# A token loop on one core: turning y on VectorE, and the float32 products of a chunk in two groups instead of four

## The chip, the cores and the metric

The program runs on one core of a Trainium2 chip. A core has TensorE (PE: matrix products, with PEld for its weight loads), VectorE (DVE), ScalarE (ACT), GpSimd (POOL) and SyncE (SP, which here only issues DMAs). Each engine works through its own instructions strictly in order and waits at an instruction until the semaphores that it needs are set. The metric is the time of one execution on the device in microseconds (us), the median of several runs.

## The reference

Three stages follow each other; x has 8 sequences of 3072 rows of 256 numbers, so 24576 tokens in all.

```
X = rfft(x over the sequence);  Y = shrink(X @ (w_r + i w_i) + b);  y = irfft(Y)      # y: 24576 x 256
h = y @ w_in                                   # 24576 x 2048
t = (h - tanh(h)) @ w_out                      # 24576 x 256
logits = t @ phi                               # 24576 x 32
d = softmax of logits over all tokens;  slot_input = d.T @ t
slot_out[e] = relu(slot_input[e] @ w1[e]) @ w2[e]      # 8 experts, 4 slots each
out = (softmax of logits over the slots) @ slot_out
```

## The kernel before, in words

**Three phases.** The spectral phase takes the first 700 us or so, the token phase then runs to about 2150 us, the expert phase is the rest. The change lies in the token phase.

**The token phase.** The 24576 tokens are taken in 48 chunks of 512. `w_out` is never applied to a single token: with g = tanh(h) the logits are sums of products of g and of y with folded weights (`wp`, `wy`), and slot_input is built from d.T @ g and d.T @ y, over all chunks, with a running maximum (`acc`, `accy`, `ssum`). For each chunk c the steps have short names in the table `PLAN` (lines 29 to 42), which sets the order of everything by hand; an entry is (name, offset of the chunk, arguments), and every engine gets its instructions in that order.

- `P` w n (`wino`, line 749): h is computed by a Winograd scheme, for each of four weight blocks w in seven products n = 1 to 7. One product is six matmuls (of split float32, `f32r`, three terms for each of two halves). Products 1, 6, 7 and 4 of a block add up one after the other in the same PSUM bank, and after each of the four ACT copies the bank to an SBUF tile `g` (line 782) before the next one may write to the bank. Product 2 has a bank of its own, 5 and 3 share a third. A bank is a tile `ph`; there are six.
- `A` (`add`, line 784): DVE adds a bank to a part of g (line 789). `G` (`gate`): ACT takes the tanh of a whole g tile of 128x1024 (line 793).
- `T` (`turn_g`, line 840): DVE transposes g in 32x32 blocks (line 846) into a tile `gt`, two instructions per g tile. `reg` (`regroup`, line 852): 16 DMAs from SP carry one half of a chunk's `gt` (h = 0 or 1) to four tiles `gq`, so that the tokens lie on the partitions.
- `L` p (`logit_mm`, line 885): plain float32 matmuls of g tiles p and p+1 with `wp` into the bank `pl` (line 892), and at p = 6 also those of y with `wy` (line 900).
- `TY` kk (`turn_y`, line 805): y is turned by PE, four 128x128 transposes (line 812) into the bank `pd` for each of two halves, and ACT copies the bank to the tile `yq` (line 813). `loadr` loads y again for this (tile `yr`).
- `sum`, `sum2`, `max`, `exp`, `turnexp`: the logits' maximum and exponentials; `comb`, `cexp`, `cend`: the softmax over the slots, stored by a DMA.
- `DY` and `D` (`dy_mm`, `dg_mm`): plain float32 matmuls of the turned exponentials `et` with `yq` (line 828) and with `gq` (line 1020). `accy` and `acc` add them up on DVE.

**What a chunk's turn of the plan contains.** The entries with offset -1 belong to the chunk before. In one turn PE has 28 products (168 matmuls), and among them four groups of plain float32 matmuls: L2 and L4; then L6 with y, and TY0; then TY1, and L0 of the next chunk; then DY and D. SP's DMAs come in this order: the load of y for the next chunk, the store of the softmax, the 16 DMAs of the second half (h = 1) of the chunk before, `loadr`, and the 16 DMAs of the first half (h = 0) of this chunk. Those write to `gq` tiles that D reads, and so wait in part for D.

Of the kernel before, what the change touches and what calls it, by code (L numbers as in the profile page):

```python
# [9 lines left out]
F32 = mybir.dt.float32  # L10
# [3 lines left out]
ALU = mybir.AluOpType  # L14
# [4 lines left out]
S, D = 3072, 256  # L19
# [7 lines left out]


PLAN = (
# [8 lines left out]
    ("reg", -1, 1), ("W", 0, 3), ("splitt", 1, 0), ("comb", -1), ("P", 0, 3, 7),  # L38
# [3 lines left out]
)  # L42
TOKENS_BESIDE = {-4: 1, -2: 1, 0: 1, 1: 2, 2: 3, 3: 4}
# [590 lines left out]
def token_phase(tc, nch, yd, wh, wl, wp, wy, ident, ew):  # L634
# [8 lines left out]
    nc = tc.nc  # L643
    with ExitStack() as ctx:
# [73 lines left out]
        gt = {}  # L718
        banks = count()

        def bank():
            k = next(banks) % (4 if ps2 is None else 6)
            return (ps if k < 4 else ps2).tile([128, 512], F32, tag=f"b{k}", name="ph")
# [71 lines left out]
        yr = {}  # L795
        yq = {}
# [23 lines left out]
        def dy_mm(c):  # L820


            beside = c < nch - 1
            o = dy[c] = lp[c + 1][:, 256:320] if beside else bank()[:, 0:64]
            y = yq.pop(c)
            for k in range(4):
                for a in (3, 2, 1, 0):
                    nc.tensor.matmul(  # L828
                        o[32 * a:32 * a + 32], ex[c][:, k, :], y[:, a, k], start=k == 0 and not beside, stop=k == 3,
                        skip_group_check=True,  # L830
                    )

        def accum_y(c):
# [3 lines left out]
            else:  # L837
                nc.vector.tensor_copy(accy, o)

        def turn_g(c, p):  # L840
            g = gs[c, p]
            if (c, p // 4) not in gt:
                gt[c, p // 4] = gtp.tile([128, 16, 8, 32], F32, tag="gt", name="gt")
            t = gt[c, p // 4]
            for u in range(2):
                nc.vector.transpose(out=t[:, :, 2 * (p % 4) + u, :], in_=g[:, u, :].rearrange("p (c i) -> p c i", i=32))  # L846

        gq = {}

        gl = {}  # L850

        def regroup(c, h):

            t = gt.pop((c, h)).rearrange("p (k q) f i -> p q k (f i)", q=4)
            if h == 0:
                gq[c] = [ew.gq_tile([128, 4, 512]) for _ in range(4)]
            for a in range(4):
                o = gq[c][a][:, :, 256 * h:256 * h + 256]
                for q in range(4):
                    nc.sync.dma_start(out=o[32 * q:32 * q + 32], in_=t[32 * a:32 * a + 32, q])  # L860

        def turn_pe(c, p, engines):

            if p // 4 not in gl:
                gl[p // 4] = gtp.tile([128, 4, 4, 256], F32, tag="gt", name="gl")
            o = gl[p // 4].rearrange("p k a (f i) -> p k f a i", i=32)
            for u in range(2):
                t = bank()
                for k in range(4):
                    k = slice(128 * k, 128 * k + 128)  # L870
                    nc.tensor.transpose(t[:, k], gs[c, p][:, u, k], ident)
                src = t.rearrange("p (k a i) -> p k a i", k=4, a=4)
                dst = o[:, :, 2 * (p % 4) + u]
                if engines[u] is nc.scalar:
                    nc.scalar.activation(dst, src, AF.Copy)
                else:
                    engines[u].tensor_copy(dst, src)
# [51 lines left out]
        ex = {}  # L929
# [34 lines left out]
        def turn_exp(c):  # L964
            e, rs, a = le[c][64:128], rss.pop(c), al.get(c)
            et = sp.tile([128, 4, 32], F32, tag="et", name="et", bufs=1)
            for r in range(2):
                nc.vector.transpose(
                    out=et[64 * r:64 * r + 64].rearrange("p k s -> p (k s)"), in_=e[:, 128 * r:128 * r + 128]
                )  # L970
            if c:
                nc.vector.scalar_tensor_tensor(
                    out=ssum[0:64], in0=ssum[0:64], scalar=a[0:64], in1=rs, op0=ALU.mult, op1=ALU.add
                )
                nc.vector.tensor_copy(a[64:128], a[0:64])
            else:
                nc.vector.tensor_copy(ssum[0:64], rs)
            ex[c] = et
# [31 lines left out]
        def dg_mm(c):  # L1010

            o = dp[c] = ps2.tile([128, 512], F32, tag="d", name="pd")
            if c < nch - 1:
                parts = [(slice(0, 512), gq.pop(c))]
            else:
                parts = [(slice(256 * h, 256 * h + 256), [gl[h][:, :, a] for a in range(4)]) for h in range(2)]
            for f, g in parts:
                for k in range(4):
                    for a in (3, 2, 1, 0):
                        nc.tensor.matmul(  # L1020
                            o[32 * a:32 * a + 32, f], ex[c][:, k, :], g[a][:, k], start=k == 0, stop=k == 3
                        )
            del ex[c]
# [14 lines left out]
        gtp = ew.gtp  # L1038
# [5 lines left out]
        def do(name, k, *args):  # L1044
            if (name, k, *args) not in done:
                done.add((name, k, *args))
                calls[name](k, *args)
# [2 lines left out]
            "P": wino, "A": add, "G": gate, "T": turn_g, "L": logit_mm, "D": dg_mm, "acc": accum, "sum": sum_l,  # L1050
            "sum2": sum_l2, "max": soft_max, "exp": soft_exp, "turnexp": turn_exp, "comb": combine,
            "cexp": combine_exp, "cend": combine_end, "loady": load_y, "rawt": raw_t, "splity": split_y,
            "lowy": low_y, "splitt": split_t, "reg": regroup, "loadr": load_raw, "TY": turn_y, "DY": dy_mm,
            "accy": accum_y,
        }

        def chunk(c):

            for name, d, *args in PLAN:
                k = c + d  # L1060
                if name == "S":

                    if c == 1:
                        split_sw(*args)
                elif name == "W":
                    if c == nch - 1:
                        weights(*args)
                elif k > 0 and k < nch or k == 0 and name not in "PAG":
                    if k < nch - 1 or name not in ("T", "reg"):
                        if c < nch - 1 or name not in ("D", "DY", "accy"):  # L1070
                            do(name, k, *args)
                    if c == 1 and (name, k, *args) == ("L", 0, 4):
                        do("L", 0, 6)

        def weights(w):

# [17 lines left out]
        c = 0  # L1094
        for s in range(8):
            p = FIRST[s]
            if s == 3:
                ew.open_mid()
            if s == 5:
                ew.open_late()  # L1100
                acc, accy, ssum = ew.acc, ew.accy, ew.ssum
# [33 lines left out]
        c = nch - 1  # L1135
# [59 lines left out]
class ExpertWeights:  # L1195
# [61 lines left out]

    def load_ct(self, c0, c1):
        n = c1 - c0
        u = self.gtp.tile([128, n, 128], F32, tag="gt", name="ect") if c0 else self.gq_tile([128, n, 128])  # L1260
        for c in range(c0, c1, 16):
            m = min(c + 16, c1)
            self.tc.nc.sync.dma_start(out=u[:, c - c0:m - c0], in_=self.ctd[:, c:m])
        for c in range(c0, c1, 8):
            self.cts[c] = u[:, c - c0:c - c0 + 8]
# [5 lines left out]
    def pieces(self, j, home):  # L1271
        def tile(pool, tag, n=1024, **kw):
            t = pool.tile([128, n], F32, tag=tag, name="ewt", **kw)
            return [t[:, 512 * i:512 * i + 512] for i in range(n // 512)]
# [9 lines left out]
        if home[0] == "s":  # L1284
            return tile(self.tyq, home, 1536)
        if home == "gt":
            r = tile(self.gtp, "gt", 4096)
            self.spare["gt"] = r[4:]
            return r[:4]
        if home == "gq":  # L1290
            t = self.gq_tile([128, 2048])
# [205 lines left out]
```

## Time and profile before

| | |
|---|---|
| median of 3 runs | 2262.81 us (2259.74 to 2264.0) |
| the profiled execution | 2261.4 us, of which the span is 2259.6 us |
| mean granted TensorE clock | 0.993 |
| PE, DVE, ACT, POOL busy | 98%, 78%, 64%, 29% of the span |
| DMA packets, share of 16 engines | 77.6% |

A share is an average over the whole span. The profile says what one execution did; busy PE counts modelled ends of pipelined matmuls, so two matmuls that follow each other at 0.12 us each show 0.28 us. What a matmul costs is therefore read from the distance of starts, or from a whole piece of the chain.

### The profile page before, as it was taken

To read this page: it belongs to the slowest core of one execution; us is meant where nothing else is said; L and a number is where in the kernel's file an instruction comes from. 1 tells how busy PE (TensorE), PEld (TensorE's weight loads), DVE (VectorE), ACT (ScalarE), POOL (GpSimd) and SP (SyncE) were. 2 spreads that over 40 slices of the span, in tenths; PEclk is the share of its full clock that TensorE was granted. 3 is DMA by queue.
4 is the path that set the end of the run, shared out by engine and by line. 5 is a ranking of instruction groups with operands and counts; after the bars stand their busy time and mean duration, and the time that the engine had idled before them with its cause. 6 is when DMAs were issued, how large, how long until landed. Compare 5 with 4: busy or idle time off the path is not lost.

```text
span 2259.6 us, 51262 instructions
## 1 busy us (share of the span) xinstructions
PE 2210.0 (98%) x19832; PEld 1819.3 (81%) x19832; DVE 1764.8 (78%) x3557; ACT 1456.5 (64%) x2395; POOL 656.5 (29%) x666
## 2 busy tenths in 40 slices
PE   6999999999999999999999999999999999999989
PEld 3678888887888888888888888888888888888747
DVE  3999988988995787787777877877778778777634
ACT  2456666666556677777766777676767676767524
POOL 1334333443443322222222222222222222222111
PEclk8999999999999999999999999999999999999999
DMA  8778899898657777777777777778777777777899
GB/s 227 233 226 264 250 267 277 245 261 269 201 186 211 179 168 178 179 181 181 184 172 176 175 178 179 178 180 189 171 177 177 175 179 177 182 186 173 243 341 366
DMA packets 404019, 471.17 MB, mean 209 GB/s; under 512 B 36160, under 2 KB 351808, under 8 KB 403392
## 3 DMA queue, kind: packets, MB, share of 16 engines
q1 hardware_dynamic: 403664, 467.85, 77.6%
q8 instruction: 157, 2.57, 0.5%
q14 instruction: 86, 0.70, 0.1%
q10 hardware_dynamic: 112, 0.04, 0.0%
HBM read 164.45 MB, written 106.17 MB: 120 GB/s over the span
## 4 chain that ended last, share of the span: by engine, by line
PE 87%; DVE 5%; DMA 4%; issue 2%; SPq 1%; ACT 0%; POOL 0%; DVEq 0%; POOLq 0%; ACTq 0%
PE ph L771 41%; PE pl L892 8%; PE pd L1020 8%; PE pmix L322 5%; PE pi L407 4%; PE pf L248 4%; PE pf L281 3%; PE p_out L1319 3%; PE pi L379 3%; PE pa L322 2%; PE pd L812 2%; DMA ewt<-in_moe_w 1%; PE pl L828 1%; DVE sw L372 1%; PE pl L900 1%
## 5 line engine op out<-in xcount | busy, mean ns | idle before, releaser
L782 ACT ACTIVATE g<-ph 128x512 f32<-128x512 f32 x752 | 448.0, 596 | 379.5 <-PE ph L771 354.5
L789 DVE TENSOR_TENSOR g<-ph,g 128x512 f32<-128x512 f32 x564 | 373.3, 676 | 157.7 <-PE ph L771 147.2
L846 DVE STREAM_TRANSPOSE gt<-g 128x512 f32<-128x512 f32 x752 | 476.2, 681 | 13.0 <-DMA gq<-gt 6.5
L771 PE MATMUL ph<-th,s 128*128 128x256 f32 x2256 | 482.0, 286 | 2.1 <-ACT g L782 2.1
L771 PEld LDWEIGHTS ph<-th,s 128*128 128x128 f32 x2256 | 377.8, 189 | 41.4 <-issue 19.4
L793 ACT ACTIVATE g<-g 128x1024 f32<-128x1024 f32 x376 | 392.2, 1053 | 1.5
L771 PE MATMUL ph<-tl,s 128*128 128x256 f32 x1128 | 318.3, 282 | 0.0
L771 PE MATMUL ph<-y,wh 128*128 128x256 f32 x1128 | 316.4, 280 | 0.0
L771 PE MATMUL ph<-yh,wl 128*128 128x256 f32 x1128 | 315.7, 280 | 0.0
L771 PE MATMUL ph<-yh,wh 128*128 128x256 f32 x1128 | 315.7, 280 | 0.0
L684 POOL TENSOR_TENSOR tl<-tr,th 128x512 fp32r<-128x512 f32 x94 | 121.8, 1297 | 383.8 <-ACT th L683 350.3
L372 POOL TENSOR_TENSOR sw<-t,c 64x256 f32<-64x256 f32 x192 | 169.5, 883 | 170.1 <-DVE c L364 131.3
L771 PEld LDWEIGHTS ph<-tl,s 128*128 128x128 f32 x1128 | 213.9, 190 | 0.0
L771 PEld LDWEIGHTS ph<-yh,wh 128*128 128x128 f32 x1128 | 212.8, 189 | 0.1
L771 PEld LDWEIGHTS ph<-yh,wl 128*128 128x128 f32 x1128 | 212.4, 188 | 0.0
L771 PEld LDWEIGHTS ph<-y,wh 128*128 128x128 f32 x1128 | 212.3, 188 | 0.1
L678 POOL TENSOR_TENSOR tr<-y 128x256 f32<-128x256 f32 x92 | 67.8, 737 | 470.3 <-DMA y<-yd 470.3
L892 PE MATMUL pl<-g,wp 128*32 128x256 f32 x3072 | 195.4, 383 | 0.0
L1020 PE MATMUL pd<-gq,et 128*32 128x512 f32 x1504 | 183.8, 598 | 2.1 <-DMA gq<-gt 2.1
L669 POOL TENSOR_TENSOR y<-y,yh 128x1024 fp32r<-128x1024 f32 x46 | 110.6, 2403 | 182.9 <-issue 182.8
L407 PEld LDWEIGHTS pi<-i,v 96*128 96x128 f32 x1024 | 127.5, 191 | 26.0 <-issue 20.8
L281 PEld LDWEIGHTS pf<-f,a 128*128 128x128 f32 x768 | 102.5, 195 | 54.3 <-issue 40.9
(225 smaller groups left out, 4586.0 us busy)
## 6 DMA issues: line engine op xcount, KB each, us to landing
gq<-gt SPq DMA_DIRECT2D x1504, 128.0 KB, 2.5
xt<-in_x SPq DMA_DIRECT2D x64, 384.0 KB, 5.4
vd<-vs SPq DMA_DIRECT2D x96, 256.0 KB, 3.3
v<-vd SPq DMA_DIRECT2D x64, 384.0 KB, 5.4
yd<-yt SPq DMA_DIRECT2D x48, 512.0 KB, 5.6
y<-yd SPq DMA_DIRECT2D x48, 512.0 KB, 4.9
yr<-yd SPq DMA_DIRECT2D x48, 512.0 KB, 3.7
a<-ad SPq DMA_DIRECT2D x47, 512.0 KB, 6.0
```

The costliest lines, as they stand in the source:

```text
L281: nc.tensor.matmul(p[:, :, h, gg, :], t[:, gg, 128 * h:128 * h + 128], f2[:, 128 * g:128 * g + 128], start=True, stop=True,)
L322: nc.tensor.matmul(o, st[u], w[m], start=first and k == 0, stop=last and k == 2)
L372: eng.tensor_tensor(out=v[64 * ri:64 * ri + 64, gg], in0=t[q, e], in1=c[q, e], op=ALU.subtract)
L407: nc.tensor.matmul(p[:, a, :], t[:, 4 * u + a, :], i2[:, 96 * n2:96 * n2 + 128], start=True, stop=True)
L684: nc.gpsimd.tensor_tensor(out=lo, in0=t, in1=hi.bitcast(F32), op=ALU.subtract)
L771: nc.tensor.matmul(o[:, 256 * j:256 * j + 256], a[u][:, 128 * j:128 * j + 128], y[v], start=new and j == 0 and k == 0, stop=n in (2, 3, 4) ...
L782: nc.scalar.activation(e[n], o.rearrange("p (j n) -> p j n", j=2), AF.Copy)
L789: nc.vector.tensor_tensor(out=h, in0=o, in1=h, op=ALU.add)
L793: nc.scalar.activation(g, g, AF.Tanh)
L846: nc.vector.transpose(out=t[:, :, 2 * (p % 4) + u, :], in_=g[:, u, :].rearrange("p (c i) -> p c i", i=32))
L892: nc.tensor.matmul(lp[c][q:q + 32, 0:256], wp[:, 2 * p + f, :], half_of(gs[c, p + f // 2][:, f % 2], h), start=p == 0 and f < 2, stop=Fals ...
L1020: nc.tensor.matmul(o[32 * a:32 * a + 32, f], ex[c][:, k, :], g[a][:, k], start=k == 0, stop=k == 3)
```

## The change

`turn_y` is no longer called in the loop (it stays for the last chunk). A new step `TD` (`turn_yr`) transposes y on DVE in 32x32 blocks into two more places of the tile `gt` of the second half, which grows from 8 to 10 places; the second half's 16 DMAs carry 320 instead of 256 numbers a row, and `DY` reads its y from the tail of the `gq` tiles. The two `gt` tiles get names and one buffer each, where they took turns in two buffers. In the plan L2, L4 and L6 now stand together behind product (1, 2), and L0 stands directly ahead of DY and D. One `scalar_tensor_tensor` on a 64x1 operand becomes a `tensor_scalar`. The SBUF space that is put aside for dynamic DMAs is set to 1024.

```diff
 PLAN = (
-    ("P", 0, 0, 6), ("cend", -2), ("L", -1, 2), ("T", -1, 4), ("T", -1, 7), ("G", -1, 6), ("loady", 1), ("W", 0, 0), ("L", -1, 4),
+    ("P", 0, 0, 6), ("cend", -2), ("T", -1, 4), ("T", -1, 7), ("TD", -1), ("G", -1, 6), ("loady", 1), ("W", 0, 0),
...
-            y = yq.pop(c)
+            if beside:
+                y = [g[:, :, 512:576] for g in gq[c]]
+            else:
+                y = [yq[c][:, a] for a in range(4)]
...
+        def gt_tile(c, h):
+            if (c, h) not in gt:
+                gt[c, h] = gtp.tile([128, 16, 8 + 2 * h, 32], F32, tag=f"gt{h}", name="gt", bufs=1)
+            return gt[c, h]
+
+        def turn_yr(c):
+
+            t = gt_tile(c, 1)
+            for kk in range(2):
+                nc.vector.transpose(out=t[:, :, 8 + kk, :], in_=yr[c][:, kk].rearrange("p (c i) -> p c i", i=32))
...
             if h == 0:
-                gq[c] = [ew.gq_tile([128, 4, 512]) for _ in range(4)]
+                gq[c] = [ew.gq_tile([128, 4, 576]) for _ in range(4)]
             for a in range(4):
-                o = gq[c][a][:, :, 256 * h:256 * h + 256]
+                o = gq[c][a][:, :, 256 * h:256 * h + 256 + 64 * h]
...
             if c:
-                nc.vector.scalar_tensor_tensor(
-                    out=ssum[0:64], in0=ssum[0:64], scalar=a[0:64], in1=rs, op0=ALU.mult, op1=ALU.add
+                nc.vector.tensor_scalar(
+                    out=ssum[0:64], in0=ssum[0:64], scalar1=a[0:64], scalar2=rs, op0=ALU.mult, op1=ALU.add
                 )
...
-                    if c == 1 and (name, k, *args) == ("L", 0, 4):
-                        do("L", 0, 6)
...
-    nc = bacc.Bacc("TRN2", target_bir_lowering=False, num_devices=1)
+    nc = bacc.Bacc("TRN2", target_bir_lowering=False, num_devices=1, dynamic_dma_scratch_size=1024)
```

**PE at the head of a turn.** Names with numbers are tiles; `ph_16653` is the bank of products 1, 6, 7 and 4 of block 0. Before, product 6, then L2 and L4 (`pl`), then the start of product 7:

```order
L771 MATMUL ph_16653<-th_16577,s_7815 128x256 [waits Activation_49]
L771 MATMUL ph_16653<-tl_16578,s_7815 128x256
L771 MATMUL ph_16653<-th_16577,s_7815 128x256 x2
L771 MATMUL ph_16653<-tl_16578,s_7815 128x256
L771 MATMUL ph_16653<-th_16577,s_7815 128x256
L892 MATMUL pl_16514<-g_16339,wp_77 32x256 [waits DVE_49]
L892 MATMUL pl_16514<-g_16339,wp_77 32x256 x3
L892 MATMUL pl_16514<-g_16383,wp_77 32x256 x4
L892 MATMUL pl_16514<-g_16394,wp_77 32x256 x4
L892 MATMUL pl_16514<-g_16482,wp_77 32x256 x4
L771 MATMUL ph_16653<-th_16649,s_7815 128x256 [waits Activation_49]
L771 MATMUL ph_16653<-tl_16650,s_7815 128x256 [waits Pool_49]
```

In the changed kernel the same place, with `ph_15610` for that bank:

```order
L771 MATMUL ph_15610<-th_15525,s_7815 128x256 [waits Activation_49]
L771 MATMUL ph_15610<-tl_15526,s_7815 128x256
L771 MATMUL ph_15610<-th_15525,s_7815 128x256 x2
L771 MATMUL ph_15610<-tl_15526,s_7815 128x256
L771 MATMUL ph_15610<-th_15525,s_7815 128x256
L771 MATMUL ph_15610<-th_15606,s_7815 128x256 [waits Activation_49]
L771 MATMUL ph_15610<-tl_15607,s_7815 128x256 [waits Pool_49]
L771 MATMUL ph_15610<-th_15606,s_7815 128x256 x2
L771 MATMUL ph_15610<-tl_15607,s_7815 128x256
L771 MATMUL ph_15610<-th_15606,s_7815 128x256
```

The 32 logit matmuls that stood between products 6 and 7 are gone from there; product 7 writes to the bank behind product 6 directly.

**PE at blocks 1 and 2.** Before, the end of product 1 of block 2 (`ph_16804`), then L6 with y and the four transposes of TY0, then product 4 of block 1, whose bank `ph_16749` product 7 of block 1 had filled ahead of these rows:

```order
L771 MATMUL ph_16804<-yh_16502,wh_85 128x256
L771 MATMUL ph_16804<-y_16311,wh_85 128x256
L771 MATMUL ph_16804<-yh_16502,wl_93 128x256
L892 MATMUL pl_16514<-g_16492,wp_77 32x256 x4
L892 MATMUL pl_16514<-g_16593,wp_77 32x256 x4
L900 MATMUL pl_16514<-yr_16662,wy_78 32x256 [waits DMAHW6_49]
L900 MATMUL pl_16514<-yr_16662,wy_78 32x256 x3
L812 MATMUL pd_16826<-ident_72,yr_16662 128x128 [waits DVE_49]
L812 MATMUL pd_16826<-ident_72,yr_16662 128x128 x3
L771 MATMUL ph_16749<-th_16649,wh_88 128x256 [waits Activation_49]
L771 MATMUL ph_16749<-tl_16650,wh_88 128x256
```

In the changed kernel the last matmul of that product 7 (`ph_15692`), product 1 of block 2 (`ph_15775`) and the start of product 4:

```order
L771 MATMUL ph_15692<-th_15606,s_7867 128x256
L771 MATMUL ph_15775<-yh_15465,wh_85 128x256 [waits DVE_49]
L771 MATMUL ph_15775<-y_15273,wh_85 128x256
L771 MATMUL ph_15775<-yh_15465,wl_93 128x256
L771 MATMUL ph_15775<-yh_15465,wh_85 128x256
L771 MATMUL ph_15775<-y_15273,wh_85 128x256
L771 MATMUL ph_15775<-yh_15465,wl_93 128x256
L771 MATMUL ph_15692<-th_15606,wh_88 128x256 [waits Activation_49]
L771 MATMUL ph_15692<-tl_15607,wh_88 128x256
```

One product of six matmuls now stands between products 7 and 4 of block 1. In the same way products 1 and 6 of block 3, which had product 5, TY1 and L0 between them, now have product 5 alone.

**DVE at the end of a turn.** Before: `accy`, the first transposes into the second half's `gt`, the last two adds of block 3, and the first row of `cend`:

```order
L836 SCALAR_TENSOR_TENSOR accy_7776<-accy_7776,al_17722,pl_17765 128x64 [waits PE_49]
L846 STREAM_TRANSPOSE gt_17897<-g_17733 128x16x32 [waits DMAHW4_49,DMAHW3_49,DMAHW5_49,DMAHW2_49,DMAHW6_49,DMAHW1_49,DMAHW7_49,DMAHW0_49,Activation_49]
L846 STREAM_TRANSPOSE gt_17897<-g_17733 128x16x32
L789 TENSOR_TENSOR g_17743<-ph_17805,g_17743 128x2x256
L789 TENSOR_TENSOR g_17743<-ph_17746,g_17743 128x2x256 [waits PE_49]
L1000 TENSOR_REDUCE cz_17959<-lt_17832 128x4 [waits Activation_49]
```

In the changed kernel, with `yr_16025` for y:

```order
L839 SCALAR_TENSOR_TENSOR accy_7776<-accy_7776,al_15840,pl_15957 128x64 [waits PE_49]
L858 STREAM_TRANSPOSE gt_16009<-g_15851 128x16x32 [waits DMAHW4_49,DMAHW3_49,DMAHW5_49,DMAHW2_49,DMAHW6_49,DMAHW1_49,DMAHW7_49,DMAHW0_49,Activation_49]
L858 STREAM_TRANSPOSE gt_16009<-g_15851 128x16x32
L789 TENSOR_TENSOR g_15861<-ph_15908,g_15861 128x2x256
L852 STREAM_TRANSPOSE gt_16009<-yr_16025 128x16x32 [waits DMAHW3_49]
L852 STREAM_TRANSPOSE gt_16009<-yr_16025 128x16x32
L789 TENSOR_TENSOR g_15861<-ph_15864,g_15861 128x2x256 [waits PE_49]
L1012 TENSOR_REDUCE cz_16073<-lt_15935 128x4 [waits Activation_49]
```

The two transposes of y stand between the two adds of block 3, and the first of them waits for the load of y.

## Rows read from the trace of the kernel before

**Rows 1.** Token phase: length, busy PE, PEld, DVE, ACT, POOL, clock, DMA share, GB/s.

```profile
740.00:2120.00 1380.00, 1380.00 (x14316) 1159.14 (x14314) 1088.94 (x2244) 975.23 (x1561) 356.54 (x317) 1.00 0.75 178
```

**Rows 2.** The chain, one turn of the plan: start us, us, what.

```profile
1498.03 3.75 PE ph L771 x30
1501.78 1.86 PE pl L892 x32
1503.64 6.58 PE ph L771 x54
1510.22 1.00 PE pl L892 x16
1511.22 0.43 PE pl L900 x8
1511.65 0.59 PE pd L812 x4
1512.24 5.68 PE ph L771 x48
1517.93 0.44 PE pd L812 x4
1518.36 1.00 PE pl L892 x16
1519.36 4.46 PE ph L771 x36
1523.83 0.58 PE pl L828 x32
1524.41 3.69 PE pd L1020 x32
```

**Rows 3.** Groups of PE by line: busy us, mean ns, idle before: TY.

```profile
L812 PE MATMUL pd<-ident,yr 128*128 128x128 f32 x376 | 58.9, 279 | 0.0
```

**Rows 4.** Timeline, PE and ACT: the end of product 6 and its copy.

```profile
1501.50 0.28 PE L771 MATMUL ph<-th,s 128*128 128x256 f32 x1
1501.81 0.60 ACT L782 ACTIVATE g<-ph 128x512 f32<-128x512 f32 x1
```

**Rows 5.** Timeline, PE and ACT: a place in the second turn where PE waited.

```profile
731.87 0.28 PE L771 MATMUL ph<-yh,wl 128*128 128x256 f32 x1
732.80 0.59 ACT L782 ACTIVATE g<-ph 128x512 f32<-128x512 f32 x1
733.44 0.38 PE L771 MATMUL ph<-th,s 128*128 128x256 f32 x1 [1.29 <-ACT g L782]
733.66 0.28 PE L771 MATMUL ph<-tl,s 128*128 128x256 f32 x1
```

**Rows 6.** Timeline, ACT in blocks 1 and 2: tanh, copies, the logits' copy.

```profile
1510.05 1.05 ACT L793 ACTIVATE g<-g 128x1024 f32<-128x1024 f32 x1
1511.00 0.59 ACT L782 ACTIVATE g<-ph 128x512 f32<-128x512 f32 x1
...
1512.77 0.37 ACT L920 ACTIVATE le<-pl 64x256 f32<-64x256 f32 x1
1513.03 0.59 ACT L782 ACTIVATE g<-ph 128x512 f32<-128x512 f32 x1
```

**Rows 7.** The page: DVE's transposes, all turns.

```profile
L846 DVE STREAM_TRANSPOSE gt<-g 128x512 f32<-128x512 f32 x752 | 476.2, 681 | 13.0 <-DMA gq<-gt 6.5
```

**Rows 8.** Timeline, DVE: the changed small operation, and the second add of block 3.

```profile
1520.35 0.99 DVE L972 SCALAR_TENSOR_TENSOR ssum<-ssum,al,rs 64x1 f32<-64x1 f32 x1
...
1530.45 0.69 DVE L789 TENSOR_TENSOR g<-ph,g 128x512 f32<-128x512 f32 x1 [2.12 <-PE ph L771]
```

**Rows 9.** Timeline, SP: the second half's 16 DMAs.

```profile
1507.31 11.22 SPq L860 DMA_DIRECT2D gq<-gt  x16
```

**Rows 10.** The page: DMA issues, last the us from issue to landing.

```profile
gq<-gt SPq DMA_DIRECT2D x1504, 128.0 KB, 2.5
```

**Rows 11.** The same view, 1.5 us with only regrouping DMAs.

```profile
1501.00:1502.50 1.50, 1.50 (x23) 1.11 (x25) 0.72 (x5) 1.40 (x4) 0.46 (x1) 1.00 0.88 208
```

More of the change, by code (lines that the diff above doesn't have):

```diff
@@ L828, in dy_mm @@
                     nc.tensor.matmul(
-                        o[32 * a:32 * a + 32], ex[c][:, k, :], y[:, a, k], start=k == 0 and not beside, stop=k == 3,
+                        o[32 * a:32 * a + 32], ex[c][:, k, :], y[a][:, k], start=k == 0 and not beside, stop=k == 3,
                         skip_group_check=True,
@@ L838, in accum_y @@
                 nc.vector.tensor_copy(accy, o)
+        def gt_tile(c, h):
[6 more added lines that the diff above has]
+                nc.vector.transpose(out=t[:, :, 8 + kk, :], in_=yr[c][:, kk].rearrange("p (c i) -> p c i", i=32))
         def turn_g(c, p):
             g = gs[c, p]
-            if (c, p // 4) not in gt:
-                gt[c, p // 4] = gtp.tile([128, 16, 8, 32], F32, tag="gt", name="gt")
-            t = gt[c, p // 4]
+            t = gt_tile(c, p // 4)
             for u in range(2):
@@ L864, in turn_pe @@
             if p // 4 not in gl:
-                gl[p // 4] = gtp.tile([128, 4, 4, 256], F32, tag="gt", name="gl")
+                gl[p // 4] = gtp.tile([128, 4, 4, 256], F32, tag=f"gt{p // 4}", name="gl", bufs=1)
             o = gl[p // 4].rearrange("p k a (f i) -> p k f a i", i=32)
@@ L1013, in dg_mm @@
             if c < nch - 1:
-                parts = [(slice(0, 512), gq.pop(c))]
+                parts = [(slice(0, 512), [g[:, :, 0:512] for g in gq.pop(c)])]
             else:
@@ L1052, in token_phase @@
             "cexp": combine_exp, "cend": combine_end, "loady": load_y, "rawt": raw_t, "splity": split_y,
-            "lowy": low_y, "splitt": split_t, "reg": regroup, "loadr": load_raw, "TY": turn_y, "DY": dy_mm,
+            "lowy": low_y, "splitt": split_t, "reg": regroup, "loadr": load_raw, "TY": turn_y, "TD": turn_yr, "DY": dy_mm,
             "accy": accum_y,
@@ L1068, in chunk @@
                 elif k > 0 and k < nch or k == 0 and name not in "PAG":
-                    if k < nch - 1 or name not in ("T", "reg"):
+                    if k < nch - 1 or name not in ("T", "TD", "reg"):
                         if c < nch - 1 or name not in ("D", "DY", "accy"):
                             do(name, k, *args)
-                    if c == 1 and (name, k, *args) == ("L", 0, 4):
-                        do("L", 0, 6)
         def weights(w):
@@ L1259, in load_ct @@
         n = c1 - c0
-        u = self.gtp.tile([128, n, 128], F32, tag="gt", name="ect") if c0 else self.gq_tile([128, n, 128])
+        u = self.gtp.tile([128, n, 128], F32, tag="gt1", name="ect", bufs=1) if c0 else self.gq_tile([128, n, 128])
         for c in range(c0, c1, 16):
@@ L1286, in pieces @@
         if home == "gt":
-            r = tile(self.gtp, "gt", 4096)
+            r = tile(self.gtp, "gt0", 4096, bufs=1)
             self.spare["gt"] = r[4:]
```

10 rows, old and new, of the table PLAN are left out of this document.

## The prediction, made before the changed kernel was run

> **What bounds the kernel now.** I read the busy time by stage first. In 1380 us of the token phase PE is busy for 1380, DVE for 1089, ACT for 975 [rows 1], so PE is the bound there and has no gap that another engine could fill or open. Next the chain: over one turn of the plan, from 1498.03 to 1524.41 + 3.69 = 1528.10, it is PE alone, 30.07 us [rows 2]. The reader should see four stretches of products ("ph") and between them the four groups of plain float32 matmuls. The stretch of 48 matmuls takes 5.68 us, 0.118 each, so a product of six takes 0.71; the stretches that follow a group end up longer: 3.75 for 30 is 0.20 over 30 x 0.118, and 6.58 for 54 is 0.19 over [rows 2]. That 0.19 is what PE pays to come back from a group. Whatever shortens PE's work shortens a turn, as long as PE still finds nothing to wait for; there are 376 / 8 = 47 turns with a TY [rows 3].
>
> **What the change takes from PE.** The two groups of four transposes cost 0.59 and 0.44, together 1.03 us a turn [rows 2]. With them goes one return of 0.19 (of the four, the stretch behind TY0, 5.68, shows none of its own). L2, L4 and L6 in one group may run at the 1.86 / 32 = 0.058 each of the first group where the lone groups of 16 show 1.00 [rows 2], 0.07 less for each of L6 and L0. So a turn loses between 1.03 + 0.19 = 1.22 and 1.22 + 0.14 = 1.36 us; I take 1.30. Over 47 turns that alone is 61 us.
>
> The Trainium skill, page "TensorE: Matmul & The Clock Gate", section "Part 4: PE-mode transpose", gives about 275 ns for a 128x128 transpose inside a kernel. The rows here show 279 ns for one as a duration, but four within 0.44 to 0.59 us, since they overlap [rows 2, 3]; the piece of the chain is what a turn gets back.
>
> **What the change makes PE wait for.** The groups did a second job: they stood between products that write to one bank. Product 6's result must be copied by ACT before product 7 writes to the same bank. Before, L2 and L4 (1.86 us) cover that copy; in the new order product 7 of block 0 follows product 6 directly. Its price comes from two places. The last matmul of product 6 starts at 1501.50, its copy at 1501.81 and takes 0.60 [rows 4]: the copy ends 0.91 after that start, and ACT does the same work ahead of it as before. Where PE did wait for a copy, the copy ended at 732.80 + 0.59 = 733.39, PE began at 733.44, 0.05 later, and its next matmul came at 733.66, 0.22 behind instead of 0.12 [rows 5]: 0.10 more. So product 7 in effect starts 0.91 + 0.05 + 0.10 = 1.06 after the last start, where 0.12 would do: 0.94 us lost.
>
> The same rule holds at two more places. Between products 7 and 4 of block 1 stood product 1 of block 2 and the group L6, y and TY0; now only that product, 0.71. Between products 1 and 6 of block 3 stood product 5 and the group TY1, L0; now only product 5. Each loses 0.94 - 0.71 = 0.23, if ACT is free when the bank is ready. Product 4 of block 0 still has two products and the new group behind product 7, and every other pair has two products or more, 1.42, which covers the 0.94. Sum: 0.94 + 0.23 + 0.23 = 1.40 us a turn.
>
> ACT is in order too, and the pauses of the second and third group are gone from the long stretch of 20 products. The tightest place is product 7 of block 2, which waits for product 6's copy. From the end of product 7 of block 1 to there, ACT has four copies of 0.59, two tanh of 0.95 (1510.05 to 1511.00) and the logits' copy of 0.26 (1512.77 to 1513.03) [rows 6], 4.52 us, less where neighbours overlap. With 0.31 ahead and 0.15 behind that is 4.98; PE takes 0.12 + 6 x 0.71 + 0.23 = 4.61. ACT is late by 0.37 at most, and by nothing if the copies overlap by 0.1 each as rows 6 show for the tanh (1.05 long, followed after 0.95). I take 0.10. The stretch loses no further tanh, and ACT loses two copies of y.
>
> **What DVE and the DMAs take on.** Two transposes of 0.68, 1.36 us a turn [rows 7], stand between the last two adds of block 3. The second of these waited 2.12 us for PE [rows 8], and the new work fits into that wait. They need the new load of y, which goes out right behind the second half's DMAs, at 1518.5 or so [rows 9], while they come after DY and D, towards 1528 [rows 2]. The small operation of 0.99 [rows 8] becomes cheaper by something between nothing and nearly all of it; it lies in the stretch where DVE is busiest, so it only pays for part of the transposes. Without the cover DVE would be late by up to 1.36 at the end of a turn, on the add that product 2 of block 1 waits for; four products lie in between.
>
> The second half's 16 DMAs take 11.22 us of issue from 1507.31 [rows 9], so the last goes out at 1518.53 and lands 2.5 later [rows 10], at 1521.0; DY starts at 1523.83 [rows 2]. That is 2.8 us of slack. DY came 25.8 us behind the last D; in the new order it is 19.9 of products, 0.4 of returns, 3.3 of the first group, 0.9 of L0 and 1.5 of waits, 26.0, so the slack stays (without the waits it would be 1.3 to 1.5). With 320 instead of 256 numbers a row the DMAs may cost nothing more, if issue sets their pace, or a quarter more engine time: the engines are busy for 0.88 of the issue time [rows 11], 0.88 x 1.25 = 1.10, so up to 0.10 x 11.22 = 1.1 us later. Both are inside the slack; cost nothing, with 0 to 0.3 if the landing also slows.
>
> On this the Trainium skill speaks against the change: "DMA: Bandwidth & Descriptors", section "How a descriptor splits into AXI transactions", says that an aligned descriptor becomes one transaction for each 256 B, so 1280 B would be five where 1024 B are four. By that rule the upper end of the last paragraph would hold, and the sum would still be the same; no row here shows a 1280 B row.
>
> The buffers with names of their own change nothing: each half used every second buffer before. The space for dynamic DMAs shows in no row of an engine; cost nothing.
>
> **The sum.** A turn: -1.30 + 1.40 + 0.10 = +0.20 us. Over 47 turns +9.4 us. On the profiled execution's 2261.4 us that is 2270.8, and the median of the runs lies 1.4 above that execution: 2272. The likeliest case has its own bounds: -1.36 + 1.40 = +0.04 a turn, 2 us, to -1.22 + 1.40 + 0.37 = +0.55, 26 us: 2265 to 2289.
>
> **The rivals.**
> Faster: the waits don't come, because the copy of product 6 is not waited for at the start of product 7, or ACT starts it before the product's last matmul. Then a turn keeps its 1.30, 61 us, and the time is 2202. For it: the chain shows PE without a single wait at these places [rows 2]. Against it: product 7 adds to what product 6 left in the bank while the copy needs the sum without it, and rows 5 show PE standing for 1.29 us in just such a case. It decides at the head of the turn: a wait below 0.8 there brings the sum below zero. A weaker form, half of the waits, gives -0.6 a turn, 2235.
> Faster by another price: were a transpose worth the 279 ns of its row [rows 3], eight would give back 2.23 instead of 1.03, and a turn would change by -1.00, 47 us: 2216. The page on TensorE named above, with its 275 ns, would lead there. Against it stand the pieces of 0.59 and 0.44.
> No change: the lower bound of the sum, +0.04 a turn, or up to +0.1: 2263 to 2267. ACT's overlaps then hide the place in block 2, and the groups lose their extra 0.14.
> Much slower: ACT becomes the bound in the long stretch. If a tanh comes in front of a copy at one of the two places where one product is left, 0.95 is added there, 45 us: 2317. For it: ACT's 4.5 us of work against PE's 4.6. Against it: the tanh ahead of product 7's copy in block 1 follows product 6's copy at once and has two products' time, 1.42, for its 0.95; and ahead of the other place ACT has only the short exponentials and one copy. Late DMAs at DY would be a second way, some 0.3 a turn.
>
> **How the numbers follow.** The waits with the sum of +0.1 a turn or more: 0.58. No change: 0.25. Faster, all forms: 0.12. Much slower: 0.05. No change means within 0.2%, 4.5 us, about what a measurement of this kernel can tell. Faster by over 0.2% takes the 0.12 and a little of the no-change case, 0.13; within 0.2%: 0.27; slower: 0.60. The range goes from 2257, so that it holds the no-change case and the weakest gains, to 2289, the upper bound of the likeliest case.
>
> **What would show it.** In the changed profile PE should have, in every turn, a wait on ACT's copy (line 782) of about 0.8 us in front of product 7 of block 0, and two of about 0.1 to 0.2 in blocks 1 to 3; the group of L2, L4 and L6 about 2.8 us long, with y 0.43; no "pd" with ident before the last chunk; turns of about 30.3 us; PE busy below its 1380 of 1380. DVE should show the two transposes of y with no wait for `yr` and no wait of PE on DVE; DY no wait on a DMA. The forecast is wrong if turns come out at 29 us (no waits), or if PE waits for DVE or for `gq`.

## The result, and the profile after

The changed kernel took 2286.41 us (median of 4 runs, 2280.33 to 2290.77) against 2263.4 us before (2259.74 to 2266.32): a ratio of 1.0106 with a 95% interval of 1.0090 to 1.0123, so slower by 1.1%. The forecast was 2272 us, in a range of 2257 to 2289. The direction and the range held, but the time was not spent where the forecast put it. The profiled execution took 2280.3 us (span 2278.6), the fastest of the four, 19 us more than the one before; what follows accounts for that one. All times here are medians of executions at a granted clock of 0.99; one of e8_no_copy_waits at 0.75 (2633.47 us) is left out of its figure.

The token phase by stage, as in [rows 1]; PE is now busy for 1332 of 1380 us, with DVE as busy as before:

```profile
740.00:2120.00 1380.00, 1332.31 (x13752) 1091.99 (x13744) 1094.37 (x2307) 907.16 (x1441) 354.57 (x315) 1.00 0.82 192
```

What PE waited for in that stretch (engine, line <- who: us in total, times, longest); before the list was empty:

```profile
PE ph L771 <- ACT g L782: 30.9, 45, 0.7
PE pl L831 <- DMA gq<-gt: 10.5, 10, 3.0
PE pl L831 <- DVE lt L998: 2.2, 2, 1.1
PE pl L831 <- DVE g L789: 2.1, 3, 0.8
PE pl L831 <- DVE cm L1002: 1.4, 1, 1.4
```

The first row is the forecast wait on product 6's copy, 0.69 in each of 45 turns. The others, with one of 0.4 that is not shown, are waits in front of DY, 16.6 us together. A wait for several semaphores is put down to the one that came last; the three DVE rows name transposes, a maximum and an add that DY does not read. The landings in the trace show that they are waits for `gq` too: behind 15 of the 17 waits DY starts 0.09 to 0.25 us after the last wide DMA has landed.

The chain of one quiet turn, answering to [rows 2] (start, us, what):

```profile
1503.07 3.75 PE ph L771 x30
1506.82 0.02 issue
1506.85 0.60 ACT g L782
1507.45 0.04 issue
1507.50 2.40 PE ph L771 x18
1509.89 2.73 PE pl L904 x48
1512.62 0.43 PE pl L912 x8
1513.05 15.09 PE ph L771 x120
1528.14 1.00 PE pl L904 x16
1529.14 0.49 PE pl L831 x29
1529.63 3.43 PE pd L1032 x32
```

It ends at 1533.06: 29.99 us, against 30.07 before. The four groups took 9.59 us, the two take 8.08; the stretches of products took 20.47 and take, with the wait, 21.9. So the saved work and the waits on copies cancel, 0.1 us a turn in the change's favour. But only some turns are like this. The distance from one D to the next was 29.97 to 30.21 before, in all turns but the last; now it goes from 29.95 to 33.31, and the sum over 46 turns is 22 us longer. A slow turn of the same execution shows why (SP's issues, then the chain):

```profile
1601.57 1.42 SPq L658 DMA_DIRECT2D y<-yd  x1
1603.08 12.05 SPq L872 DMA_DIRECT2D gq<-gt  x16
```

```profile
1614.36 7.65 DMA gq<-gt
1622.02 0.09 issue
1622.11 0.82 PE pl L831 x29
```

The last wide DMA goes out at 1614.36 and lands 7.65 us later, and DY starts then. The page's DMA rows, answering to [rows 10] (which has both halves in one), show the median landing of the wide DMAs and of the first half's narrow ones; a landing is counted from the start of the DMA's issue:

```profile
gq<-gt SPq DMA_DIRECT2D x752, 160.0 KB, 4.6
gq<-gt SPq DMA_DIRECT2D x752, 128.0 KB, 2.4
```

DY needs the last of the 16, and there the two kernels part. Below are the second half's first two DMAs and its last three in the turn of [rows 9], before (last number: us to landing); then the same in the slow turn above:

```profile
gq<-gt SPq DMA_DIRECT2D x2, 128.0 KB, 3.5
gq<-gt SPq DMA_DIRECT2D x3, 128.0 KB, 2.4
```

```profile
gq<-gt SPq DMA_DIRECT2D x2, 160.0 KB, 6.0
gq<-gt SPq DMA_DIRECT2D x3, 160.0 KB, 6.2
```

Over all turns of each trace, the median landing falls from 4.7 us at the first of the 16 to 2.5 at the last before, and only from 4.8 to 4.1 in the changed kernel. Both series start with a lag, right behind the load of y (0.5 MB); the narrow one works it off and the wide one does not. The issue of all 16 takes 12.63 us in the median turn and took 11.37. In the packet records of this trace's token phase (740 to 2120 us) a row of 1280 B took 94 ns (median of 92160) and one of 1024 B 71 (92672); in the kernel before the second half's rows of 1024 B took 73.

On DVE all went as hoped, answering to [rows 8]: the transposes of y fill the wait of the second add, and the small operation takes 0.27 for 0.99.

```profile
1496.15 0.27 DVE L984 TENSOR_SCALAR ssum<-ssum,al,rs 64x1 f32<-64x1 f32 x1
...
1503.34 1.28 DVE L852 STREAM_TRANSPOSE gt<-yr 128x512 f32<-128x512 f32 x2
1505.42 0.69 DVE L789 TENSOR_TENSOR g<-ph,g 128x512 f32<-128x512 f32 x1 [0.80 <-PE ph L771]
```

### The profile page after: what moved, and what is told of

Read it like the earlier page. It is cut to its first block, busy times and chain, and to the rows that moved or that the text cites. A ratio compares the mean times of both kernels' runs of the same rounds, so it can differ in the third digit from the quotient of the medians.

```text
span 2278.6 us, 50416 instructions
## 1 busy us (share of the span) xinstructions
PE 2181.9 (96%) x19456; PEld 1770.3 (78%) x19456; DVE 1786.2 (78%) x3651; ACT 1403.9 (62%) x2301; POOL 657.0 (29%) x666
## 4 chain that ended last, share of the span: by engine, by line
PE 46%; SPq 9%; DMA 6%; DVE 5%; ACT 2%; issue 1%; DVEq 0%; ACTq 0%
PE ph L771 29%; SPq L872 8%; PE pd L1032 7%; PE pl L904 5%; DMA gq<-gt 3%; PE p_out L1329 3%; DVE gt L858 2%; DMA ewt<-in_moe_w 2%; PE pl L831 1%; DVE g L789 1%; ACT g L782 1%; PE pl L912 1%; DMA gq<-wo 0%; SPq L1018 0%; ACT g L793 0%
## 5 line engine op out<-in xcount | busy, mean ns | idle before, releaser
L904 PE MATMUL pl<-g,wp 128*32 128x256 f32 x3072 | 185.9, 382 | 0.0
L1032 PE MATMUL pd<-gq,et 128*32 128x512 f32 x1504 | 173.2, 595 | 0.0
```

The lines of the kernel that those rows point to most:

```text
L904: nc.tensor.matmul(lp[c][q:q + 32, 0:256], wp[:, 2 * p + f, :], half_of(gs[c, p + f // 2][:, f % 2], h), start=p == 0 and f < 2, stop=Fals ...
L1032: nc.tensor.matmul(o[32 * a:32 * a + 32, f], ex[c][:, k, :], g[a][:, k], start=k == 0, stop=k == 3)
```

## The experiments

Two theories stood against each other. The DMA theory: the wide DMAs land late, and DY waits for them. The rival: VectorE (or ScalarE) is late in the new order, or the waits on copies are the price.

**e1_narrow: the wide DMAs taken away.** From the changed kernel:

```diff
-gq[c] = [ew.gq_tile([128, 4, 576]) for _ in range(4)]
+gq[c] = [ew.gq_tile([128, 4, 512]) for _ in range(4)]
-o = gq[c][a][:, :, 256 * h:256 * h + 256 + 64 * h]
+o = gq[c][a][:, :, 256 * h:256 * h + 256]        # and the source cut to 0:256
-y = [g[:, :, 512:576] for g in gq[c]]
+y = [g[:, :, 0:64] for g in gq[c]]
```

Expected: 

> The changed kernel with the second half's DMAs back at 256 numbers a row and gq tiles of 512; DY reads 64 columns of g in place of y, so that y's share of slot_input is left out. VectorE still turns y, the plan is untouched. DMA theory (the wide DMAs land late and DY waits for them in some turns; the waits on product copies and the saved work on TensorE cancel to -0.1 us a turn): no wait in front of DY, turns of 29.97 us throughout, 2263 - 5 - 2 = 2256 us (2250 to 2262). Rival (VectorE with 1.36 us more a turn is late at the end of a turn, TensorE waits for it): the DMAs' width changes nothing, 2280 to 2287 us.

Measured: 2271.01 us, 1.0045 of before (1.0030 to 1.0061). No wait in front of DY is left, nor in front of D, which is the one that needs the second half's DMAs here, as DY reads columns of the first half. All turns but the last are 30.19 to 30.30 us long. What PE still waits for is product 6's copy, 30.9 us in 45 waits up to 2100 us, as in the changed kernel.

The rival falls: VectorE does the same work and nobody waits for it. But the time is 15 us above what the DMA theory gave, 11 of them because a turn is 30.21 and not 29.97. The chain shows the piece that differs, D, 3.67 where the changed kernel has 3.43:

```profile
1527.76 1.00 PE pl L904 x16
1528.76 0.45 PE pl L831 x32
1529.21 3.67 PE pd L1032 x32
```

**e2_before_wide: the wide DMAs alone, in the kernel before.** Its plan and TensorE's turning of y stay; `TD` and the 320 numbers are added, with the changed kernel's `gt` tiles and space for dynamic DMAs, which e1 has too:

```diff
-("A", 0, 3, 2), ("P", 0, 3, 3)
+("A", 0, 3, 2), ("TD", 0), ("P", 0, 3, 3)
-o = gq[c][a][:, :, 256 * h:256 * h + 256]
+o = gq[c][a][:, :, 256 * h:256 * h + 256 + 64 * h]
```

Expected: 

> The kernel before, its plan and TensorE's turning of y kept, and added to it VectorE's two transposes of y at the end of a turn and the second half's DMAs with 320 numbers a row (what they carry of y is not read). TensorE's work and order are those of before. DMA theory: the last wide DMA lands about 4 us later than the narrow one did, against 2.8 us of slack at DY and 3.3 at D, so D waits for gq in a good part of the turns: 2268 to 2295 us. Rival (VectorE late, only in the new order): the transposes fit into the 2.1 us wait, 2262 to 2266 us, no wait at D.

Measured: 2288.99 us, 1.0123 (1.0102 to 1.0144). Quiet turns stay at 30.07, others reach 32.64, and PE waits at D (up to 2100 us):

```profile
PE pd L1029 <- DMA gq<-gt: 16.4, 15, 2.4
```

The wide DMAs alone cost as much as the whole change. VectorE's transposes are in this kernel too, but e1 has them without the DMAs and without a wait.

**e3_moved: the wait on product 6's copy taken away.** From the changed kernel:

```diff
-("G", -1, 6), ("loady", 1), ("W", 0, 0),
+("G", -1, 6), ("loady", 1), ("W", 0, 0), ("L", -1, 2), ("L", -1, 4), ("L", -1, 6),
-("P", 0, 1, 2), ("L", -1, 2), ("L", -1, 4), ("L", -1, 6), ("P", 0, 0, 4)
+("P", 0, 1, 2), ("P", 0, 0, 4)
```

Expected: 

> The changed kernel with L2, L4 and L6 moved from behind product (1, 2) to between products (0, 6) and (0, 7); all else the same. The wait of 0.69 us (0.94 with the return) on product 6's copy must go. DMA theory: TensorE comes to DY about 0.9 us earlier in every turn and waits there for the wide DMAs instead, so at most a third of 43 us is gained: 2270 to 2286 us, waits in front of DY of 25 to 60 us in sum. Rival (the copy wait is the price): all of it is gained, 2286 - 43 = 2243 us (2236 to 2252).

Measured: 2291.43 us, 1.0127 (1.0098 to 1.0156): nothing gained. The copy wait is gone; the waits in front of DY grew from 15.6 to 45 us (both up to 2100 us), of which these are the largest:

```profile
PE pl L831 <- DMA gq<-gt: 21.2, 20, 2.9
PE pl L831 <- DVE lt L998: 8.5, 8, 1.2
PE pl L831 <- DVE cm L1002: 7.1, 5, 1.6
```

Not all of this is TensorE coming earlier. With the group ahead of product 7, the add that waits for product 7's copy comes later on VectorE, and so do the transposes behind it that the wide DMAs carry: the first wide DMA goes out 11.0 us after D's end instead of 10.3 (medians over the turns), 0.03 us behind the end of a transpose. So the edit also delayed the DMAs by some 0.7 us a turn, and how much of the 0.94 it would gain without that was not tried.

**e4_narrow_moved: both edits together.**

Expected: 

> Both edits together: DMAs of 256 numbers (DY reads 64 columns of g, y's share of slot_input is left out) and L2, L4, L6 between products (0, 6) and (0, 7). DMA theory: with the DMAs out of the way TensorE's side shows in full: turns of 29.97 - 0.94 = 29.03 us, 2256 - 43 = 2213 us (2206 to 2224). Rival (VectorE late): no better than 2240 us.

Measured: 2226.12 us, 0.9844 (0.9826 to 0.9862). Turns are 29.25, 0.96 below e1's. So the copy wait is worth 0.96 a turn, as forecast (0.94), once the DMAs are out of the way, and nothing in e3, where they are in it. Of the 13 us above the expected 2213, 11 are again D's 3.67. What is left in the long stretch of products:

```profile
1515.90 17.22 PE ph L771 x138
1533.12 1.00 PE pl L904 x16
1534.12 0.45 PE pl L831 x32
1534.57 3.67 PE pd L1032 x32
```

138 x 0.118 and the return of 0.19 make 16.5; 0.70 are short waits. The starts of the matmuls show where. In the changed kernel's quiet turn product 4 of block 1 loses 0.26 us, product 6 of block 3 0.24 and product 7 of block 2 0.18, each behind a copy by ACT: 0.68 for the prediction's 0.23, 0.23 and 0.10.

**e8_no_copy_waits: the short waits, too.** From e4:

```diff
-("P", 0, 1, 4), ("S", 0, 3)
+("P", 0, 2, 2), ("P", 0, 1, 4), ("S", 0, 3)        # and (2, 2) gone from its place, two entries behind sum2
-("P", 0, 3, 6), ("turnexp", -1), ("T", 0, 3), ("P", 0, 2, 3)
+("turnexp", -1), ("T", 0, 3), ("P", 0, 2, 3), ("P", 0, 3, 6)
```

Expected: 

> The kernel of e4_narrow_moved (y's share of slot_input left out, DMAs of 256 numbers) with products (2, 2) ahead of (1, 4) and (2, 3) ahead of (3, 6). The two short waits on copies and what follows from them must go. By the prediction's 0.23 + 0.23 + 0.10 a turn: 0.56, 2226 - 26 = 2200 us; by the 0.70 that the long stretch of the changed kernel is over its 120 matmuls: 2194 us; together 2188 to 2206. Rival (VectorE or ScalarE bound at 29.2 us a turn): 2220 us or more.

Measured: 2229.74 us, 0.9853 (0.9837 to 0.9870), turns of 29.33: no gain, the rival's side. The chain shows two new breaks in the stretch:

```profile
1514.39 7.99 PE ph L771 x66
1522.38 0.01 issue
1522.39 4.72 PE ph L771 x36
1527.11 0.04 issue
1527.15 4.53 PE ph L771 x36
```

Together 17.29 for 138 again. The first break is product 6 of block 2, which waits for the copy of product 1; that copy (1521.75 to 1522.34 on ACT) stands behind a tanh that began at 1520.80. At the second, product 3 of block 2, now earlier, meets VectorE's add. An earlier product only met ScalarE and VectorE elsewhere; whether another order of their work would do better was not tried.

**e5_three_groups and e6_two_groups_pe: the grouping without y on VectorE.** From the kernel before, with product (2, 3) ahead of (3, 6) in both, and (2, 2) ahead of (1, 4) and acc ahead of cend in e6:

```diff
e5: -("L", -1, 6), ("TY", -1, 0), ("sum", -1)            +("TY", -1, 0), ("L", -1, 6), ("TY", -1, 1), ("sum", -1)
    -("TY", -1, 1), ("L", 0, 0), ("lowy", 1)             +("lowy", 1)
    -("P", 1, 0, 2), ("DY", -1), ("D", -1)               +("P", 1, 0, 2), ("L", 0, 0), ("DY", -1), ("D", -1)
e6: -("L", -1, 4),                                       +("L", -1, 4), ("TY", -1, 0), ("L", -1, 6), ("TY", -1, 1),
    # and TY0, L6, TY1 gone from their places, L0 ahead of DY as in e5
```

Expected: 

> The kernel before, TensorE still turning y, DMAs narrow; only the plan differs: TY0, L6 with y, TY1 in one group, L0 directly ahead of DY and D, and product (2, 3) ahead of (3, 6) so that two products stand between 1 and 6 of block 3. DMA theory: one return of 0.19 and 0.14 of the lone L groups are saved in each turn, nothing waits: 2261 - 15 = 2246 us (2240 to 2254), turns of 29.75 us. Rival (fewer pauses make ScalarE and VectorE late): 2258 us or more, TensorE waiting for copies.

Expected: 

> The kernel before with all of it in two groups, TensorE still turning y and DMAs narrow: L2, L4, TY0, L6 with y, TY1 between products (0, 6) and (0, 7); L0, DY, D as the other group; acc ahead of cend; products (2, 2) and (2, 3) ahead of (1, 4) and (3, 6), so that every pair on one bank has two products or a group between. DMA theory: the two returns of 0.38 and 0.14 are saved, 0.52 a turn, no waits: 2261 - 24 = 2237 us (2229 to 2247), turns of 29.55 us. Rival (ScalarE or VectorE late in the long stretch): 2255 us or more.

Measured: 2277.53 us, 1.0063 (1.0048 to 1.0078), and 2286.42 us, 1.0100 (1.0084 to 1.0117). Both times fell on the rival's side. Fewer groups alone lose: e6's chain has the groups at 9.70 us where the kernel before had 9.59, and the products, broken like e8's, at 20.83 for 20.47.

```profile
1527.16 4.71 PE ph L771 x36
1531.87 0.04 issue
1531.91 4.52 PE ph L771 x36
...
1537.88 3.78 PE pd L1020 x32
```

In e5 the groups cost 9.77, since TY0 as the first of a group takes 0.66 and TY1 at the end 0.59; that is 0.18 of the 0.26 us that a turn is longer, so most of its loss is not the rival's lateness. How much of it each edit of these two plans costs was not separated.

**e7_d_first: what makes D 0.25 us faster.** From e6:

```diff
-("L", 0, 0), ("DY", -1), ("D", -1), ("accy", -1)
+("L", 0, 0), ("D", -1), ("DY", -1), ("accy", -1)
```

Expected: 

> The kernel of e6_two_groups_pe with D ahead of DY. In the kernel before D stands behind DY and has four or five waits for DMA queues of 51 ns each on TensorE's queue in front of it, and its group is 0.25 us longer than in the changed kernel, where these waits stand behind L0. If it is these waits that L0's queued matmuls hide, D ahead of DY hides them too: 0.25 a turn, 2237 - 11 = 2226 us (2219 to 2234). If the changed kernel's faster D comes from the gq tiles' row pitch of 576 numbers, nothing changes: 2237 us.

Measured: 2269.65 us, 1.0036 (1.0025 to 1.0047), 16.8 us below e6 (0.33 a turn). D takes 3.43, with narrow DMAs and gq rows of 512 numbers, so the row pitch is not it:

```profile
1529.02 3.43 PE pd L1020 x32
```

The theory of the waits on TensorE's queue held: the trace has 235 such entries of 51 ns in front of D in the kernel before, 189 in e1, none in front of the changed kernel's loop D, whose waits stand at DY behind L0.

**e9_before_d_first: that alone, in the kernel before.** One swap in its plan, `("D", -1), ("DY", -1)` for `("DY", -1), ("D", -1)`.

Expected: 

> The kernel before with one swap in the plan: D ahead of DY. D's waits for DMA queues (five of 51 ns a turn on TensorE's queue) then stand behind a product of six matmuls of 0.118 us instead of behind DY's 32 matmuls of 15 ns each. If queued matmuls hide such waits, as D behind L0 showed (3.43 us instead of 3.78), D's group is 0.25 us shorter in each of 46 turns: 2261.7 - 11.5 = 2250 us (2246 to 2255), turns of 29.82 us. If they hide nothing here: 2262 us.

Measured: 2251.36 us, 0.9948 (0.9934 to 0.9962): the fastest complete kernel here, ahead of both. All turns but the last take 29.83 or 29.84.

```profile
1518.36 3.57 PE pd L1020 x32
1521.93 0.45 PE pl L828 x32
```

Group 4 is 4.02 long where [rows 2] had 0.58 + 3.69 = 4.27. Whichever of the two comes first behind a product pays about 0.13 for it (DY 0.58 for 0.45, D 3.57 for 3.43), so the 0.25 saved is what the waits cost.

**e10_y_early: relief for the wide DMAs.** From e3, with y's load between the first half's 8th and 9th DMA, and one turn earlier:

```diff
-("G", -1, 6), ("loady", 1), ("W", 0, 0)
+("G", -1, 6), ("W", 0, 0)
-("P", 0, 3, 3), ("A", 0, 3, 3),
+("P", 0, 3, 3), ("A", 0, 3, 3), ("loady", 2), ("reg2", 0),      # reg sends 8, reg2 the other 8
```

Expected: 

> The changed kernel as in e3_moved (L2, L4, L6 between products (0, 6) and (0, 7)), with one transfer moved in SP's order: the load of y for the next turns goes out between the first half's 8th and 9th DMA, one turn earlier than it did, and no longer directly ahead of the wide DMAs. By the chain theory a turn of e3_moved is the sum D's end, 12 DMAs of the first half, store and load (9.3 us), 16 wide DMAs (13.2), landing (3.7), DY and D (4): 30.2 us; without the load ahead of the wide ones their engines start free of its 0.5 MB, about 1 us, and SP is free 0.1 to 0.4 earlier: turns of 29.2 to 30.0, 2291 - 30 = 2261 us (2245 to 2280). If the total of bytes is the limit and not the chain, nothing changes: 2285 to 2295 us.

Measured: 2262.56 us, 0.9993 (0.9981 to 1.0005), 29 us below e3 with not a byte less. The load of y now stands among the narrow DMAs:

```profile
1498.55 0.54 SPq L658 DMA_DIRECT2D y<-yd  x1
1499.13 5.51 SPq L874 DMA_DIRECT2D gq<-gt  x8
...
1506.28 11.86 SPq L874 DMA_DIRECT2D gq<-gt  x16
```

Counted from D's end, the wide DMAs start as in e3 (11.0 us, medians over the turns), but their issue takes 11.9 us for 12.8, and the first lands 2.6 us after it goes out, not 4.0. PE still waits in front of DY, 21.8 us up to 2080 us (13.4 of them put down to `gq`), and a turn takes 29.24 to 31.29. The order of the transfers, not the sum of bytes alone, sets that price. The edit also sends the load a turn earlier and splits the narrow DMAs; these parts were not separated.

## Why the prediction was right in its range and wrong in its reason

- *The bound.* Right: PE filled 1380 of 1380 us before, and what lengthened the phase are PE's waits.
- *The gain of 1.30 us a turn.* The pieces gave 1.51: TY 1.03 as forecast, the L pieces 0.13 as forecast, DY and D 0.35, which was not forecast; the return of 0.19 is in the stretches of products. Of the 0.35, some 0.25 are D's queue waits (e7, e9).
- *The wait on product 6's copy, 0.94.* Right. The trace shows 0.69 as idle; e4 against e1 gives 0.96 a turn with the return.
- *The two short waits and ACT's lateness, 0.56.* Right: the three places show 0.68, the long stretch is 0.70 over. That they can be taken away by two products in between, as the prediction's rule has it, did not hold: in e8 the products met ACT and DVE elsewhere.
- *The sum, +0.20 a turn and 2272 us.* It is the sum of e1, where the DMAs are narrow: +0.13 a turn and 2271.0 us. In the changed kernel, D's waits are hidden as well and the sum is -0.1.
- *The step that failed.* "Both are inside the slack; cost nothing, with 0 to 0.3 if the landing also slows." The term for the landing was mis-sized. The issue of the 16 came out about as bounded: 12.63 us for 11.37 in the median turn, 1.3 for at most 1.1 (the quiet turn's 13.20 holds one issue of 2.19). But the last DMA landed 4.0 us after it went out instead of 2.5 (medians), 1.5 for at most 0.3, and up to 7.7. Together that is the whole slack: the last landing lay 2.65 us ahead of DY before (median, 1.3 to 3.8) and lies 0.46 ahead now, and in 17 turns up to 2120 us PE waits for it. What the step left out is the lag at the start of the series. Its own 0.88 x 1.25 = 1.10 said that the engines cannot keep up with the issue; it charged the issue for that and let the landing stay near 2.5, as if the 16 started on empty queues. They start behind the load of y, with a landing of 4.8, and with 1.10 that is not worked off. e10, without the load ahead, starts at 2.6.
- *The slack of 2.8.* Near the median by luck. The 2.5 of [rows 10] counts from the start of an issue and was added to the end of the last one; the turn that was read had 3.5, others as little as 1.3.
- *A row's price.* The bound took 1.25 from the bytes. The rows show 94 ns for 71 in one execution, 1.32, or for 73 before, 1.29. The Trainium skill, "DMA: Bandwidth & Descriptors", "How a descriptor splits into AXI transactions", would give five transactions for four, 1.25; the measured factor lies a little above it.
- *The 19 us of the profiled execution.* They are this term: waits of 16.6 us in front of DY up to 2120 us and one of 2.8 after it, and 0.25 more for DY and D behind each wait (4.24 us up to the next product, where a quiet turn has 3.99), less the quiet turns' gain of 0.1.
- *Luck.* What the prediction counted comes out at -0.1 a turn in this kernel. That the time is above before, and inside the range, is the work of the term that it put at nothing. By its own sign, "if PE waits for DVE or for `gq`", the forecast is wrong.
- *The rivals.* The two faster forms are refuted: the copy wait came in every turn, and TY gave back 1.03, not 2.23. "Late DMAs at DY", named in one clause at 0.3 a turn, is what happened, at about 0.4 in the profiled execution and more in the others, whose median is 6 us above it. ACT as the bound came in small, as the short waits. The forecast time lay 14 us below the measured one.

## What to carry to other kernels

When a transfer is made wider, ask what is queued ahead of its series and whether the engines work that off before the last DMA, for the wait is for that one. Here rows of 1024 B worked off the lag behind a load of 0.5 MB within 16 DMAs, and rows of 1280 B did not. Groups of other work between two products on one bank are not only cost; before merging them, look at which copy each of them covers. And where an instruction waits for several DMA queues, put it behind matmuls that are long enough to keep TensorE fed while its queue works through the waits: this one swap gave 0.5%, where the larger change lost 1.1%.

## What the runs showed of the hardware that was not expected

- D's waits for several DMA queues stand as entries of 51 ns on TensorE's queue, five a turn, also when the DMAs have long landed (2.65 us before DY, median). Behind DY's 32 short matmuls they show (D's piece 3.69 to 3.78 us), behind L0 not at all (3.43). Behind a product D takes 3.57, of which some 0.14 is the start of a group behind a product.
- From SBUF to SBUF a row of 1280 B took 94 ns and one of 1024 B 71 in the same token phase (medians, under load; the fastest tenth 55 and 47 or less).
- Moving one load of 0.5 MB away from the start of the 16 wide DMAs, a turn ahead and among the narrow ones, was worth 29 us of 2291 (e10 against e3).
